# Expert weights into the keys' and values' memory: a fused attention and mixture-of-experts kernel

## Chip, cores and metric

One core of one Trainium2 chip runs the kernel. The metric is device time in microseconds (us), the median of several executions. A profiled execution has its own time, and the trace belongs to that one execution.

## What is computed

Inputs: q, k, v of 4 batches, 8 heads, 768 positions, 64 columns, float32; gate weights 512 x 8; expert weights w1 (8 x 512 x 1024) and w2 (8 x 1024 x 512); capacity 80. Attention with 4 sink positions and a window of 128 comes first, and its rows go through a router that gives each row to one expert:

```python
keep = is_sink | in_window
scores = np.where(keep, scores, -1000000000.0)
a = np.exp(scores - np.max(scores, axis=-1, keepdims=True))
a = a / (np.sum(a, axis=-1, keepdims=True) + 1e-09)
x = ...                       # rows: 3072 x 512, 8 heads side by side
expert_idx = np.argmax(x @ w_gate, axis=1)
for e in range(E):            # at most 80 rows of an expert, those of largest gate weight
    h = np.maximum(x[tok_idx] @ w1[e], 0.0)
    out[tok_idx] = gate_w[tok_idx, None] * (h @ w2[e])
```

All rows that no expert keeps are zero.

## The kernel before, in words

`attention_moe` does the work in one straight program (`any_window` is a general version behind a branch that these inputs don't take).

**Attention loop.** 48 ticks, 12 per batch. A tick takes two blocks of 128 queries by a pair of heads. Tick n computes scores on TensorE (`scores`, L504) into one PSUM bank a block; VectorE masks and takes the negated row maximum (`softmax`, L521 to L531); ScalarE takes exponentials with the row sum (`exps`, L541). One tick later the probabilities are transposed (`transposes`, L557) and copied by ScalarE (`keep_probs`, L569), GpSimd cuts them into two triangles (L577, L584), and two ticks later TensorE multiplies by the values (`weighted`, L592, L598). The sinks' values are kept in float32r with a remainder: `round_v` (L382) rounds them on ScalarE, `split_v` (L387) subtracts on GpSimd, 4 pieces a batch, in batch 0 within tick 1. The only table load of ScalarE stands ahead of its first exponential (L541).

Finished rows are turned back (L631), copied by ScalarE into one of two `xr` buffers (L636), scaled by GpSimd (L641) and stored to `x_rows` in DRAM (L645). Gate logits and keys follow, and VectorE compares each key with all earlier ones in pieces of 768 (`rank_compare`, L746, L749); this work goes on after the last tick.

**Order.** All of it is written by hand: `at(n, f)` puts a step at tick n and the loop issues the engines' instructions tick by tick. Loads and stores of the loop stand in one queue, SyncE's, which issues in order and stops at a transfer whose wait isn't over. Each transfer also waits for the one eight places ahead of it.

**Keys and values.** A batch's keys (`k`) and values (`v`) come from two rotating buffers each, in pool `ld` on the right side of memory. It closes after the last tick (`lctx.close()`, L904).

**Weights.** The 16 matrices (1 MB a half, 32 halves) are wanted in the order w1 of 0, w1 of 1, w2 of 0, w1 of 2, w2 of 1 and so on. They go to 17 places: `NA` = 6 in a pool that is there from the start, loaded from tick `W0` = 26 every `WD` = 3 ticks; `NB` = 7 in `ld`'s memory, issued together after the last tick (L905 to L908); `NC` = 4 in memory of the loop's other pools (L964 to L967). The last 15 halves replace used ones (`in_home`, L289 to L291).

**After the loop.** Ranks become row numbers (L978 to L996), GpSimd gathers each expert's 80 rows from `x_rows` (L1007), with 14 matmuls meanwhile that keep TensorE busy (L1005). Then, for expert e: `tokens` transposes its rows (L1037, copy L1039), `ffn1` multiplies by w1 (L1051, 128 matmuls: for each of 8 column groups all 4 row groups of w1), `ffn2` by w2 (L1066, 128 matmuls: for each of 4 column groups all 8 row groups), `rows` transposes back, scales and scatters to `out` (L1082 to L1094). TensorE's order is ffn1(e), tokens(e+1), rows(e-2), ffn2(e-1). A half of a weight matrix is half of its rows, so every column group reads both halves.

Of the kernel before, what the change touches and what calls it, by code (L numbers as in the profile page):

```python
# [8 lines left out]
F32 = mybir.dt.float32  # L9
F32R = mybir.dt.float32r  # L10
# [3 lines left out]
AF = mybir.ActivationFunctionType  # L14
# [5 lines left out]
B, H, S, D = 4, 8, 768, 64  # L20
# [215 lines left out]
Z0, ZD, W0, WD = 4, 1, 26, 3  # L236
# [7 lines left out]
def attention_moe(ctx: ExitStack, tc, q, k, v, n_sink, window, w_gate, w1, w2, capacity, q_t, k_t, v_t, vs_t, wg_t, out):  # L244
# [7 lines left out]
    NA, NB, NC = 6, 7, 4  # L252
# [31 lines left out]
    def load_weight():  # L284
        n = len(wtiles)
        which, e, half = wsrc[n]
        src = (w1, w2)[which][e].rearrange("(g c p) f -> g p c f", g=2, p=P)[half]

        k = n - NA - NB - NC  # L289
        in_home.append(n if k < 0 else in_home[1 + 7 * k // 4])  # L290
        pool, m = homes[in_home[n]]  # L291
        t = pool.tile([P, 2 * F], F32, tag=f"w{m}", name=f"w_{which}_{e}_{half}", bufs=1)
        nc.sync.dma_start(t.rearrange("p (c f) -> p c f", c=src.shape[1]), src)
        wtiles[(which, e, half)] = t

    zeros = const.tile([P, DM], F32, name="zeros")
    ve.memset(zeros, 0.0)

    with ExitStack() as actx:
# [60 lines left out]

        def load_k(b, pieces=1):
            ks[b] = ld.tile([P, NPAIR, NBLK * BLKW], F32, tag="k", name=f"k_{b}")
            n = NPAIR // pieces
            for i in range(pieces):
                nc.sync.dma_start(ks[b][:, i * n:(i + 1) * n], k_t[b][:, i * n:(i + 1) * n])

        def load_v(b, upto=NPB):

            if b not in vv:
                vst[b] = vst_rows[b % 2]  # L370
                vv[b] = ld.tile([P, NBLK, DM], F32, tag="v", name=f"v_{b}")
            for i in range(v_done.get(b, 0), upto):
                nc.sync.dma_start(vv[b][:, 2 * i:2 * i + 2], v_t[b][:, 2 * i:2 * i + 2])
                if i == 0:
                    nc.sync.dma_start(vst_raw, vs_t[b])
            v_done[b] = upto
# [3 lines left out]
        def round_v(b, m):  # L380
            a, hp = m // 2, slice(m % 2 * 2, m % 2 * 2 + 2)
            ac.copy(vst[b][0:SROWS, a, hp].bitcast(F32R), vst_raw[0:SROWS, a, hp])  # L382

        def split_v(b, m):

            a, hp = m // 2, slice(m % 2 * 2, m % 2 * 2 + 2)
            po.tensor_tensor(vst[b][32:SROWS, a, hp].bitcast(F32R), vst_raw[32:SROWS, a, hp], vst[b][32:SROWS, a, hp],  # L387
                             ALU.subtract)
# [9 lines left out]
        first_k = ks[0] = ld.tile([P, NPAIR, NBLK * BLKW], F32, tag="k", name="k_0")  # L398
# [380 lines left out]
        def at(n, f, *args):  # L779
            cal.setdefault(n, []).append((f, args))  # L780
# [7 lines left out]
        for n in range(NA):  # L788
            at(W0 + WD * n, load_weight)
        at((2, "pool"), make_experts)  # L790
# [13 lines left out]
        for m in range(4):  # L804
            at((1, "act mid"), round_v, 0, m)
            at((1, "pool"), split_v, 0, m)
# [50 lines left out]
        with tc.manual_schedule():  # L857
            n = 0
            while n <= END:
# [34 lines left out]
                run(n, "pe end")  # L894
                run(n, "act end")
# [6 lines left out]
                if n == END:  # L902

                    lctx.close()  # L904
                    wpool2 = fast.enter_context(tc.tile_pool(name="wpool2", bufs=1, side="right", reuse_waits="tile"))  # L905
                    homes += [(wpool2, m) for m in range(NB)]
                    for _ in range(NB):
                        load_weight()  # L908
# [54 lines left out]
    with ExitStack() as fctx:  # L963
# [7 lines left out]
        for e in range(E):  # L971
            xg[e] = sm.tile([CAP, DM], F32, name=f"xg_{e}")
# [68 lines left out]
        def ffn1(e):  # L1041
            need(0, e)
            x = xts.pop(e)
            h = wk.tile([P, HC, CAP], F32, tag="h", name=f"h_{e}")
            for half in range(2):
                ph = ps_h.tile([P, HC // 2, CAP], F32, tag="ph", name=f"ph_{e}_{half}")
                for f in range(HC // 2):
                    fc = half * (HC // 2) + f
                    for c in range(DC):
                        for m in range(2):  # L1050
                            pe.matmul(ph[m * D:(m + 1) * D, f], columns(0, e, c, fc * P + m * D),  # L1051
                                      x[:, c], start=(c == 0), stop=(c == DC - 1), skip_group_check=True)
                ac.activation(h[:, half * (HC // 2):(half + 1) * (HC // 2)], ph, AF.Relu)  # L1053
            hs[e] = h

        def ffn2(e, between=None):
# [5 lines left out]
            for dc in range(DC):  # L1062
                to = py if dc < DC // 2 else last
                for k in range(HC):
                    for m in range(2):
                        pe.matmul(to[m * D:(m + 1) * D, dc], columns(1, e, k, dc * P + m * D), h[:, k],  # L1066
                                  start=(k == 0), stop=(k == HC - 1), skip_group_check=True)
# [106 lines left out]
```

## Time and profile before

| | us |
|---|---|
| three timed executions | 322.2, 322.96, 324.96 (median 322.96) |
| the profiled execution | 321.46 |
| its span, first to last instruction | 319.7 |
| attention loop, first exponential to last tick's | 9.4 to 187 |
| ranks and row numbers | to 216.5 |
| gather, experts, last scatter | 216.5 to 319.7 |

A row of the profile names line, engine, operation, output and inputs. "issue" after an arrow is a wait for nothing that the profile shows. SPq is SyncE's queue. The granted TensorE clock stands as a share of 2.4 GHz.

### The profile page before, as it was taken

To read this page: it belongs to the slowest core of one execution; us is meant where nothing else is said; L and a number is where in the kernel's file an instruction comes from. 1 tells how busy PE (TensorE), PEld (TensorE's weight loads), DVE (VectorE), ACT (ScalarE), POOL (GpSimd) and SP (SyncE) were. 2 spreads that over 40 slices of the span, in tenths; PEclk is the share of its full clock that TensorE was granted. 3 is DMA by queue.
4 is the path that set the end of the run, shared out by engine and by line. 5 is a ranking of instruction groups with operands and counts; after the bars stand their busy time and mean duration, and the time that the engine had idled before them with its cause. 6 is when DMAs were issued, how large, how long until landed. Compare 5 with 4: busy or idle time off the path is not lost. (4 is left out here: it accounts for less than half of the span.)

```text
span 319.7 us, 11526 instructions
## 1 busy us (share of the span) xinstructions
PE 276.4 (86%) x4616; PEld 218.6 (68%) x4616; DVE 180.5 (56%) x576; ACT 159.1 (50%) x631; POOL 164.8 (52%) x365
## 2 busy tenths in 40 slices
PE   7498999999979999999999895745888989999792
PEld 2265776867767777777676673332788989998681
DVE  5345988777888989799989999970000000000001
ACT  0766897788968788777776661100111212111110
POOL 4396797769897588967667765507300111011001
PEclk9679999999999999999999999558999999999998
DMA  6999143699553899345260002999996696677501
GB/s 180 326 310 413 73 133 134 223 285 324 201 202 113 279 380 408 133 148 156 111 200 35 35 3 73 355 408 368 321 380 238 220 351 211 214 253 267 186 23 49
DMA packets 27115, 69.72 MB, mean 218 GB/s; under 512 B 2736, under 2 KB 3760, under 8 KB 26672
## 3 DMA queue, kind: packets, MB, share of 16 engines
q1 hardware_dynamic: 25744, 65.78, 59.5%
q0 software_dynamic: 1024, 2.62, 2.5%
q8 instruction: 38, 0.62, 0.8%
q10 hardware_dynamic: 288, 0.52, 0.4%
q14 instruction: 21, 0.17, 0.2%
HBM read 55.02 MB, written 13.89 MB: 216 GB/s over the span
## 5 line engine op out<-in xcount | busy, mean ns | idle before, releaser
L541 ACT ACTIVATE prob<-sc,nm 128x132 f32<-128x132 f32 (+1 forms) x192 | 69.0, 376 | 6.6 <-DVE nm L531 6.4
L504 PE MATMUL sc<-k,q 64*64 64x196 f32 (+2 forms) x768 | 48.4, 341 | 11.4 <-ACT prob L541 10.0
L1094 POOL DMA_INDIRECT out_dram<-y,idx x8 | 7.4, 921 | 81.8 <-ACT y L1083 71.6
L569 ACT COPY pt<-pp 128x512 f32<-128x512 f32 x48 | 28.1, 586 | 32.7 <-PE pp L557 24.1
L1039 DVE COPY xs<-px 128x320 f32<-128x320 f32 x8 | 3.9, 492 | 70.4 <-PE px L1037 70.4
L531 DVE TENSOR_REDUCE nm<-sc 128x2 f32<-128x264 f32 (+1 forms) x96 | 41.4, 431 | 3.3
L1051 PE MATMUL ph<-xs,w 128*64 128x80 f32 x1024 | 38.6, 233 | 5.2 <-issue 4.0
L524 DVE COPY_PREDICATED sc<-upper,sc 128x256 f32<-128x256 int8 x80 | 33.7, 421 | 14.0 <-PE sc L504 7.2
L504 PEld LDWEIGHTS sc<-k,q 64*64 64x64 f32 x768 | 21.6, 135 | 29.1 <-ACT prob L541 20.9
L1051 PEld LDWEIGHTS ph<-xs,w 128*64 128x64 f32 x1024 | 36.8, 137 | 6.4 <-issue 5.5
L1066 PE MATMUL py<-h,w 128*64 128x80 f32 x1024 | 38.4, 234 | 2.7 <-issue 2.0
L541 ACT ACTIVATION_READ_ACCUMULATOR prob<-sc,nm 128x1 f32 x192 | 40.3, 210 | 0.0
L1066 PEld LDWEIGHTS py<-h,w 128*64 128x64 f32 x1024 | 36.3, 137 | 4.9 <-issue 4.0
L598 PE MATMUL xp<-pt,v 128*64 128x128 f32 x384 | 37.5, 288 | 0.0
L577 POOL TENSOR_SCALAR_AFFINE_SELECT own<-pt 128x512 f32<-128x512 f32 (+1 forms) x48 | 28.7, 598 | 16.1 <-ACT pt L569 15.5
L749 DVE TENSOR_SCALAR_CACHE_REDUCE gt<-krow,keys 128x768 bf16<-128x768 f32 x36 | 35.5, 1004 | 0.0
L557 PE MATMUL pp<-ident,prob 128*128 128x128 f32 x192 | 32.3, 292 | 0.0
L598 PE MATMUL xp<-own,v 128*64 128x128 f32 x320 | 31.3, 274 | 0.0
L557 PEld LDWEIGHTS pp<-ident,prob 128*128 128x128 f32 x192 | 20.8, 144 | 13.9 <-issue 9.9
L1053 ACT ACTIVATE h<-ph 128x320 f32<-128x320 f32 x16 | 7.0, 438 | 44.1 <-PE ph L1051 44.1
L584 POOL TENSOR_SCALAR_AFFINE_SELECT pt<-pt 128x512 f32<-128x512 f32 (+1 forms) x48 | 27.2, 567 | 3.3
L641 POOL TENSOR_TENSOR xr<-xr,rs 128x512 f32<-128x512 f32 x24 | 25.6, 1069 | 6.0 <-ACT xr L636 5.7
(145 smaller groups left out, 461.6 us busy)
## 6 DMA issues: line engine op xcount, KB each, us to landing
w<-in_moe_w_dram SPq DMA_DIRECT2D x32, 1024.0 KB, 6.7
v<-in_v_t_dram SPq DMA_DIRECT2D x12, 512.0 KB, 7.5
out_dram<-zeros SPq DMA_DIRECT2D x24, 256.0 KB, 3.3
q<-in_q_t_dram SPq DMA_DIRECT2D x11, 512.0 KB, 7.2
x_rows<-xr SPq DMA_DIRECT2D x22, 256.0 KB, 2.2
k<-in_k_t_dram SPq DMA_DIRECT2D x3, 1584.0 KB, 9.0
k<-in_k_t_dram SPq DMA_DIRECT2D x1, 1056.0 KB, 9.7
vst_raw<-in_vs_t_dram SPq DMA_DIRECT2D x4, 256.0 KB, 6.2
```

What stands on the lines that cost most here:

```text
L504: pe.matmul(sc[u * D:(u + 1) * D, h, c0 + lo:c0 + hi], qs[g][r, hp, q0:q0 + D], ks[b][r, hp, k0 + lo:k0 + hi], start=True, stop=True, skip ...
L524: ve.copy_predicated(own, upper, sc[:, :, 0:P])
L531: ve.tensor_reduce(out=nm, in_=sc[:, :, lo_c:hi_c], axis=AX.X, op=ALU.max, negate=True)
L541: ac.activation(prob[:, a, h, p0:], sc[:, h, lo_c:hi_c], AF.Exp, bias=nm[:, h:h + 1], scale=1.0, accum_out=ssum[:, n, 2 * hp + h:2 * hp + ...
L557: pe.transpose(pp[:, a, h], prob[:, a, h, SINK:], ident)
L569: ac.copy(pt, st.pop((t, "pp")))
L577: po.affine_select(out=own[:, a0:], in_=pt[:, a0:], pattern=[[0, 2 - a0], [0, 2], [1, P]], compare_op=ALU.is_ge, fill=0.0, base=0, channel ...
L584: po.affine_select(out=pt[:, a0:], in_=pt[:, a0:], pattern=[[0, 2 - a0], [0, 2], [-1, P]], compare_op=ALU.is_gt, fill=0.0, base=0, channel ...
L598: pe.matmul(xp[h * D:(h + 1) * D, a * P:(a + 1) * P], val[:, (2 * hp + h) * D:(2 * hp + h + 1) * D], pr[:, a, h], start=False, stop=(a == ...
L749: ve.tensor_scalar(gt[:, 0:w], krow[:, c0:c0 + w], keys[:, i:i + 1], None, ALU.is_ge, ALU.add, accum_out=ra)
L1051: pe.matmul(ph[m * D:(m + 1) * D, f], columns(0, e, c, fc * P + m * D), x[:, c], start=(c == 0), stop=(c == DC - 1), skip_group_check=True)
L1066: pe.matmul(to[m * D:(m + 1) * D, dc], columns(1, e, k, dc * P + m * D), h[:, k], start=(k == 0), stop=(k == HC - 1), skip_group_check=True)
```

## The change

1. ScalarE's first instruction becomes an exponential of a zero (`first_exp`), and the table load stands ahead of that.
2. Batch 0's sink values are rounded and split on VectorE, at the end of tick 1, instead of on ScalarE and GpSimd.
3. Keys and values of a batch share one tile of a pool `kv` (two buffers). `NA` is 7 and `NB` 6: the pool from the start holds 7 halves, every 2 ticks from tick 26. Three halves go over batch 2's keys and values (tile `wkv`) at ticks 40, 42 and 44, two over batch 3's within tick 47, behind its last scores, and one after the last `weighted`. The last four (`NC`) stay where they were. To make room, the last expert's gathered rows use the tile `zeros`.
4. `ffn1` goes through all column groups with the first half of w1's rows, then with the second; `ffn2` likewise (not for the last expert). A used half is so released in the middle of a multiplication, the other at its end.

```diff
-Z0, ZD, W0, WD = 4, 1, 26, 3
+Z0, ZD, W0, WD = 4, 1, 26, 2
-    NA, NB, NC = 6, 7, 4
+    NA, NB, NC = 7, 6, 4
...
+    def kv_homes(n):
+        t = kv_tiles[B - 1] if n else kv.tile([P, NPAIR * NBLK * BLKW + NBLK * DM], F32, tag="kv", name="wkv")
+        homes.extend((None, t[:, m * 2 * F:(m + 1) * 2 * F]) for m in range(NB // 2))
...
+    first_exp = const.tile([P, 1], F32, name="first_exp")
+    ac.activation(first_exp, zeros[:, 0:1], AF.Exp)
...
+        at((NTK - 1, "act early"), kv_homes, 1)
+        for _ in range(NB // 2 - 1):
+            at((NTK - 1, "act early"), load_weight)
+
+        W1 = (B - 1) * NPB * NPAIR + 4
+        at(W1, kv_homes, 0)
+        for n in range(NB // 2):
+            at(W1 + WD * n, load_weight)
...
-        for m in range(4):
-            at((1, "act mid"), round_v, 0, m)
-            at((1, "pool"), split_v, 0, m)
+        for m in (0, 2, 1, 3):
+            at((1, "dve end"), round_v, 0, m, ve.tensor_copy)
+            at((1, "dve end"), split_v, 0, m, ve)
...
                 run(n, "pe end")
+                if n == END:
+                    load_weight()
...
-            xg[e] = sm.tile([CAP, DM], F32, name=f"xg_{e}")
+            xg[e] = sm.tile([CAP, DM], F32, name=f"xg_{e}") if e < E - 1 else zeros[0:CAP]
...
+            for c0 in range(0, DC, DC // 2):
+                for fc in range(HC):
+                    for c in range(c0, c0 + DC // 2):
+                        for m in range(2):
+                            pe.matmul(ph[fc // (HC // 2)][m * D:(m + 1) * D, fc % (HC // 2)],
+                                      columns(0, e, c, fc * P + m * D), x[:, c],
+                                      start=(c == 0 and fc % (HC // 2) == 0), stop=(c == DC - 1), skip_group_check=True)
...
+            steps = [(dc, range(k0, k0 + HC // 2)) for k0 in (0, HC // 2) for dc in range(DC)]
+            if between is not None:
+                steps = [(dc, range(HC)) for dc in range(DC)]
```

SyncE's queue from tick 42 to behind the last tick, before (`w` is a half of a weight matrix, `x_rows` a row store):

```order
L645 DMA x_rows<-xr_1_2826 128x512
L645 DMA x_rows<-xr_0_2968 128x512
L645 DMA x_rows<-xr_1_3120 128x512
L645 DMA x_rows<-xr_0_3263 128x512
L645 DMA x_rows<-xr_1_3393 128x512
L293 DMA w_2_0_3421<-in_moe_w_dram 128x2x1024
L293 DMA w_2_1_3423<-in_moe_w_dram 128x2x1024
L293 DMA w_1_0_3425<-in_moe_w_dram 128x4x512
L293 DMA w_1_1_3427<-in_moe_w_dram 128x4x512
```

The same stretch of the queue now, where `wkv` and `kv` are halves in the place of batch 2's and batch 3's keys and values:

```order
L296 DMA w_2_0_2645<-in_moe_w_dram 128x2x1024
L296 DMA wkv<-in_moe_w_dram 128x2x1024
L667 DMA x_rows<-xr_0_2772 128x512
L667 DMA x_rows<-xr_1_2833 128x512
L296 DMA wkv<-in_moe_w_dram 128x4x512
L667 DMA x_rows<-xr_0_2974 128x512
L296 DMA wkv<-in_moe_w_dram 128x4x512
L667 DMA x_rows<-xr_1_3127 128x512
L296 DMA kv_1960<-in_moe_w_dram 128x2x1024 x2
L667 DMA x_rows<-xr_0_3272 128x512
L296 DMA kv_1960<-in_moe_w_dram 128x4x512
L667 DMA x_rows<-xr_1_3403 128x512
```

Seven halves that stood behind the last row store stand ahead of it.

ScalarE's first instructions before:

```order
L541 ACT_TABLE_LOAD
L541 ACTIVATE prob_199,sum_201<-sc_108,nm_0_202 128x128 x2
L541 ACTIVATE prob_199,sum_201<-sc_109,nm_1_207 128x132 x2
L569 COPY pt_229<-pp_223 128x512
L382 CAST vst_110<-vst_raw 64x256 x4
L541 ACTIVATE prob_235,sum_201<-sc_108,nm_0_237 128x128 x2
```

And now:

```order
L311 ACT_TABLE_LOAD
L311 ACTIVATE first_exp<-zeros 128x1
L563 ACTIVATE prob_203,sum_205<-sc_113,nm_0_206 128x128 x2
L563 ACTIVATE prob_203,sum_205<-sc_114,nm_1_211 128x132 x2
L591 COPY pt_233<-pp_227 128x512
L563 ACTIVATE prob_235,sum_205<-sc_113,nm_0_237 128x128 x2
```

The four casts have gone from between the copy and tick 1's exponentials; VectorE has them, each with its subtraction, behind tick 1's maxima.

## Rows read from the trace of the kernel before

**Rows 1.** Page, part 2: the span in 40 slices, clock and DMA share
```profile
PEclk9679999999999999999999999558999999999998
DMA  6999143699553899345260002999996696677501
```

**Rows 2.** Windows: span; busy us of PE, PEld, DVE, ACT, POOL; clock, DMA, GB/s
```profile
112.00:128.00 16.00, 15.61 (x221) 11.54 (x214) 13.76 (x48) 13.58 (x56) 13.40 (x23) 1.00 1.01 393
...
180.00:198.00 18.00, 16.26 (x212) 12.71 (x204) 16.94 (x65) 9.42 (x36) 10.55 (x26) 1.00 0.09 31
```

**Rows 3.** Timeline of ScalarE, 8 to 17 us: start, duration, what, [idle before]
```profile
8.10 1.28 ACT L541 ACT_TABLE_LOAD   x1 [8.10 <-DVE nm L531]
9.40 0.37 ACT L541 ACTIVATE prob<-sc,nm 128x128 f32<-128x128 f32 x1
...
13.46 1.32 ACT L382 CAST vst<-vst_raw 64x256 fp32r<-64x256 f32 x4
14.68 0.36 ACT L541 ACTIVATE prob<-sc,nm 128x128 f32<-128x128 f32 x1
```

**Rows 4.** Timeline of VectorE, 6.5 to 17 us
```profile
8.66 0.43 DVE L531 TENSOR_REDUCE nm<-sc 128x2 f32<-128x264 f32 x1
...
16.36 0.49 DVE L521 COPY_PREDICATED_SCALAR sc<-upper,negc 128x256 f32 x1 [3.17 <-ACT stt L565]
```

**Rows 5.** Groups by form on VectorE: busy us, mean ns of one, idle before
```profile
L666 DVE TENSOR_TENSOR t<-pl,rs 128x128 f32<-128x128 f32 x11 | 3.1, 281 | 0.0
...
L983 DVE TENSOR_TENSOR hot<-slot_row,rank 128x640 bf16<-128x640 f32 x3 | 2.3, 821 | 0.0
...
L347 DVE CAST vst<-zeros 64x512 fp32r<-64x512 f32 x4 | 1.6, 472 | 0.0
```

**Rows 6.** Timeline of SyncE's queue, 196 to 210 us, weight tiles
```profile
198.22 11.50 SPq L293 DMA_DIRECT2D w<-in_moe_w_dram  x8
```

**Rows 7.** The same, 210 to 232 us
```profile
210.58 19.81 SPq L293 DMA_DIRECT2D w<-in_moe_w_dram  x4
```

**Rows 8.** Chain that ended last, from the gather on: start us, us, what
```profile
216.49 6.25 DMA xg<-x_rows,idx_in
...
233.85 0.88 issue
234.74 2.02 PE ph L1051 x52
...
237.19 2.63 PE py L1066 x71
239.82 1.21 issue
...
295.47 2.42 issue
```

**Rows 9.** DMA issues by line: the scatters of result rows; count, us to landing
```profile
out_dram<-y,idx POOLq DMA_INDIRECT x8, 3.6
```

**Rows 10.** Page, parts 1 and 3: instructions by engine; the instruction queue
```profile
PE 276.4 (86%) x4616; PEld 218.6 (68%) x4616; DVE 180.5 (56%) x576; ACT 159.1 (50%) x631; POOL 164.8 (52%) x365
...
q8 instruction: 38, 0.62, 0.8%
```

**Rows 11.** Waits of TensorE's weight loads, 223.5 to 243 us: total, times, longest
```profile
PEld ph L1051 <- issue: 3.0, 5, 1.0
PEld py L1066 <- issue: 1.4, 1, 1.4
```

**Rows 12.** The same, 243 to 302 us
```profile
PEld ph L1051 <- issue: 2.6, 1, 2.6
PEld py L1066 <- issue: 2.2, 7, 1.0
```

**Rows 13.** The same, 112 to 128 us
```profile
PEld sc L504 <- issue: 0.3, 2, 0.2
```

**Rows 14.** Timeline of SyncE's queue, 288 to 296 us
```profile
288.73 6.31 SPq L293 DMA_DIRECT2D w<-in_moe_w_dram  x3
```

More of the change, by code (lines that the diff above doesn't have):

```diff
@@ L291, in load_weight @@
         pool, m = homes[in_home[n]]
-        t = pool.tile([P, 2 * F], F32, tag=f"w{m}", name=f"w_{which}_{e}_{half}", bufs=1)
+        if pool is None:
+            t = m
+        else:
+            t = pool.tile([P, 2 * F], F32, tag=f"w{m}", name=f"w_{which}_{e}_{half}", bufs=1)
         nc.sync.dma_start(t.rearrange("p (c f) -> p c f", c=src.shape[1]), src)
         wtiles[(which, e, half)] = t
+    kv = fast.enter_context(tc.tile_pool(name="kv", bufs=2, side="right"))
+    kv_tiles = {}
+    def kv_homes(n):
+        t = kv_tiles[B - 1] if n else kv.tile([P, NPAIR * NBLK * BLKW + NBLK * DM], F32, tag="kv", name="wkv")
+        homes.extend((None, t[:, m * 2 * F:(m + 1) * 2 * F]) for m in range(NB // 2))
     zeros = const.tile([P, DM], F32, name="zeros")
     ve.memset(zeros, 0.0)
+    first_exp = const.tile([P, 1], F32, name="first_exp")
+    ac.activation(first_exp, zeros[:, 0:1], AF.Exp)
     with ExitStack() as actx:
@@ L359, in load_q, with alloc_kv @@
                 nc.sync.dma_start(qs[g][:, i * n:(i + 1) * n], q_t[g // NPB, g % NPB][:, i * n:(i + 1) * n])
+        def alloc_kv(b):
+            if b not in ks:
+                t = kv.tile([P, NPAIR * NBLK * BLKW + NBLK * DM], F32, tag="kv", name=f"kv_{b}")
+                kv_tiles[b] = t
+                ks[b] = t[:, 0:NPAIR * NBLK * BLKW].rearrange("p (h c) -> p h c", h=NPAIR)
+                vv[b] = t[:, NPAIR * NBLK * BLKW:].rearrange("p (c f) -> p c f", c=NBLK)
         def load_k(b, pieces=1):
-            ks[b] = ld.tile([P, NPAIR, NBLK * BLKW], F32, tag="k", name=f"k_{b}")
+            alloc_kv(b)
             n = NPAIR // pieces
@@ L367, in load_v @@
         def load_v(b, upto=NPB):
-            if b not in vv:
+            if b not in vst:
                 vst[b] = vst_rows[b % 2]
-                vv[b] = ld.tile([P, NBLK, DM], F32, tag="v", name=f"v_{b}")
+                alloc_kv(b)
             for i in range(v_done.get(b, 0), upto):
@@ L378, in attention_moe, with round_v, split_v @@
         v_done = {}
-        def round_v(b, m):
+        def round_v(b, m, copy=ac.copy):
             a, hp = m // 2, slice(m % 2 * 2, m % 2 * 2 + 2)
-            ac.copy(vst[b][0:SROWS, a, hp].bitcast(F32R), vst_raw[0:SROWS, a, hp])
-        def split_v(b, m):
+            copy(vst[b][0:SROWS, a, hp].bitcast(F32R), vst_raw[0:SROWS, a, hp])
+        def split_v(b, m, eng=po):
             a, hp = m // 2, slice(m % 2 * 2, m % 2 * 2 + 2)
-            po.tensor_tensor(vst[b][32:SROWS, a, hp].bitcast(F32R), vst_raw[32:SROWS, a, hp], vst[b][32:SROWS, a, hp],
+            eng.tensor_tensor(vst[b][32:SROWS, a, hp].bitcast(F32R), vst_raw[32:SROWS, a, hp], vst[b][32:SROWS, a, hp],
                              ALU.subtract)
@@ L397, in attention_moe @@
         first_q = qs[0] = ld.tile([P, NPAIR, 2 * P], F32, tag="q", name="q_0", bufs=3)
-        first_k = ks[0] = ld.tile([P, NPAIR, NBLK * BLKW], F32, tag="k", name="k_0")
+        alloc_kv(0)
+        first_k = ks[0]
         for i in range(NPAIR):
@@ L904, in attention_moe @@
                     lctx.close()
[L905 to L908, printed above, removed]
                 n += 1
@@ L1044, in ffn1 @@
             h = wk.tile([P, HC, CAP], F32, tag="h", name=f"h_{e}")
-            for half in range(2):
[L1046 to L1053, printed above, removed]
+            ph = [ps_h.tile([P, HC // 2, CAP], F32, tag="ph", name=f"ph_{e}_{half}") for half in range(2)]
+            for c0 in range(0, DC, DC // 2):
[5 more added lines that the diff above has]
+                                      start=(c == 0 and fc % (HC // 2) == 0), stop=(c == DC - 1), skip_group_check=True)
+            for half in range(2):
+                ac.activation(h[:, half * (HC // 2):(half + 1) * (HC // 2)], ph[half], AF.Relu)
             hs[e] = h
@@ L1061, in ffn2 @@
             last = ps_h.tile([P, HC // 2, CAP], F32, tag="ph", name=f"py2_{e}") if e == E - 1 else py
-            for dc in range(DC):
+            steps = [(dc, range(k0, k0 + HC // 2)) for k0 in (0, HC // 2) for dc in range(DC)]
+            if between is not None:
+                steps = [(dc, range(HC)) for dc in range(DC)]
+            for dc, some in steps:
                 to = py if dc < DC // 2 else last
-                for k in range(HC):
+                for k in some:
                     for m in range(2):
                         pe.matmul(to[m * D:(m + 1) * D, dc], columns(1, e, k, dc * P + m * D), h[:, k],
-                                  start=(k == 0), stop=(k == HC - 1), skip_group_check=True)
+                                  start=(k == 0 and (between is not None or dc == 0)), stop=(k == HC - 1),
+                                  skip_group_check=True)
                 if dc == DC // 2 - 1 and between is not None:
```

## The prediction

> **What bounds the kernel now.** I read the slices first, because the change moves transfers [rows 1]. A slice is 8 us. The DMA digits are 0 in slices 22 to 24, 168 to 192 us, and 9 in slices 26 to 30, 200 to 240 us. A window gives the empty stretch in GB/s: 31 from 180 to 198 us [rows 2]. So the loop's end leaves the memory path empty, and what follows it overfills it. The reason stands in SyncE's queue: eight weight tiles are issued from 198.22 us on, which takes 11.50 us where one issue alone takes under half a microsecond, and four more from 210.58 us [rows 6, 7].
>
> The second view is the chain of waits. From 216.49 us it is the gather of the first expert's rows, 6.25 us, and behind it TensorE alone, with pieces called "issue" between its matmuls: 0.88, 1.21 and 2.42 us are three of them [rows 8]. The weights of experts 0 and 1 have long been in memory then (loaded within the loop), so the first two are no waits for weights. Their distance says what they are. Between the ends of the 0.88 and the start of the 1.21 stand 52 + 71 matmuls and four transposes, 127 in all [rows 8]. A matmul is two instructions (a weight load and itself), which makes some 254. One DMA queue of kind "instruction" brought 38 packets, 0.62 MB, so 16 KB each [rows 10]; TensorE has 4616 matmuls and as many weight loads, 243 instructions for each packet. I read the pieces as instruction packets that come late behind weight tiles. The 2.42 us one fits: three halves were issued from 288.73 us on, within 6.31 us [rows 14].
>
> In the loop before that TensorE, VectorE and ScalarE are all nearly full (15.61, 13.76 and 13.58 of 16 us, [rows 2]), each tick waiting for the one before it. A shift of its first ticks goes through to its end; I see no transfer that holds it at a fixed time.
>
> **1. Table load and sink values.** Before, ScalarE stands until the first maximum at 8.10 us, then loads the table for 1.28 us, and the first exponential begins at 9.40 [rows 3]. With the load under the initial idle time the first begins at 8.10; but tick 0's second unit has its maximum only at 8.66 + 0.43 = 9.09 us [rows 4], against the 10.10 at which its exponential began, so what passes on is 10.10 - 9.14 = 0.96 us. The Trainium skill (ScalarE: Activation LUTs, What ACT_TABLE_LOAD costs) counts a drain of about 1.38 us on top of the load, 2.66 us in all. The rows show no such drain: 9.40 follows 8.10 + 1.28. By the page the first unit alone would gain 1.4 us more, and the second, held by its maximum, nothing.
>
> The four casts (13.46 to 14.78) stand between the probabilities' copy and tick 1's exponentials at 14.68 [rows 3]; that copy ends with the first cast's start or just behind, so some 1.1 to 1.2 us more, together 2.1. VectorE pays instead. A cast of 64x512 takes 472 ns, so 64x256 some 0.3 us; a subtraction lies between the products of 128 and of 640 columns, 281 and 821 ns, so about 0.4 [rows 5]. Four pairs are 2.8 us; the ends are 4 x (0.24 + 0.28) = 2.1, with half the cast and the smaller product, and 4 x (0.47 + 0.82) = 5.2. VectorE stood idle for 3.17 us to 16.36 [rows 4]. Shifted by 2.1 us, its next work comes at 14.3, and the pairs run from about 12 to 14.8: 0.5 us late at that point, but the next exponential waits for a copy behind TensorE's transposes, which is later still. GpSimd loses its four splits, which stood ahead of its triangles.
>
> What can eat part of it is the clock. PEclk is 6 and 7 in the second and third slice [rows 1]: TensorE runs at 1.2 GHz, half, until about 20 us, and if it rises no sooner, work pulled ahead of that point runs at half speed. About 2 us of it would cost up to 1.3. Bounds 0.7 (or minus 1, if VectorE's 5.2 decides) and 2.5; I take **1.6 us**.
>
> **2. Weights ahead.** Seven halves go from behind the last row store to ticks 38 to 49. They fall in the stretch of 31 GB/s. Seven are 7.3 MB, 19 us at the 393 GB/s of a full stretch (112 to 128 us, [rows 2]), and nothing waits for them there. Left between loop and gather are four, whose memory comes free no sooner than now: one at the end of the 11.50 us of [rows 6], three at 210.58 [rows 7], less the shift of 1.6. Three take 8 us, so they end near 217, and the gather begins at 216.49 - 1.6 = 214.9: it still meets 2 us of them, not 20.
>
> *Gather.* 6.25 us now. The scatters of equal rows, on an emptier path, land after 3.6 us [rows 9]. All of that difference would be 2.65, none of it 0. With 2 us shared, I take **1.8 us**.
>
> *Late packets, first stretch.* From 223.5 to 243 us the weight loads of TensorE wait 3.0 + 1.4 = 4.4 us for "issue" [rows 11]. About 0.8 belongs to the start (the copy of the rows). Of the 3.6 left, with a replacement tile now and then in place of twelve tiles in a row, I take 3.0.
>
> *Row halves, second stretch.* From 243 to 302 us they wait 2.6 + 2.2 = 4.8 [rows 12], of which some 0.8 are ends of a stage. The long ones follow pairs of halves released together, as at 288.73 [rows 14]. With halves released by turns, 2.3 us apart, each 1 MB has its 2.7 us nearly to itself. Not all pairs part (the last three halves still come within 8 us), so of 4.0 I take 2.6. Together **5.6 us**; the ends are 0 (packets as late as now) and 7.6. Number and kind of the matmuls stay, and the first Relu's wait moves from half to three quarters of `ffn1`, ahead of nothing that it delays.
>
> *What it could cost.* Row stores stand behind weights in the one queue. The tightest is that of tile 21, behind one half: up to 2.7 us later, and the copy of tile 23 waits for its buffer. That copy is wanted only for tile 23's own store, while VectorE still has comparisons to do, so nothing. Tick 40's tile waits for batch 2's last `weighted`, at tick 37; tick 47's two wait for scores of the same tick, and behind them stands only a row store two ticks from its use. Keys and values of batch 3 have one half more ahead of them, 2.7 us, and are used 8 ticks later.
>
> **Sum.** 1.6 + 1.8 + 5.6 = 9.0 us. The profiled execution took 321.46 (span 319.7 and 1.76 around it), which becomes 312.5. It lies 1.5 below the median of the timed ones, so I forecast 322.96 - 9.0 = 314.0 us. Its own range is 309 to 317.
>
> **Rivals.**
>
> *A. Only part of the packets are helped.* 15 of 32 halves are still loaded beside the experts, with the same bytes a microsecond from 243 on. If the second stretch keeps its 4.0 and the gather gains 0.8, what is left is 1.6 + 0.8 + 3.0 = 5.4: 317.6 us. For it: one packet meets one tile just as it meets two, by chance of phase. Against: in 243 to 302 most boundaries passed without a wait, since 14 halves left a longest wait of 2.6 and one of 1.0.
>
> *B. The "issue" pieces are something else.* The order of TensorE's own work, say, and they stay. Then start and gather remain, 3.4 us: 319.6 us. For it speaks the Trainium skill (Runtime: NRT & Kernel Launch, Instruction fetch mechanics), by which blocks of 16 KB are fetched while the one before is executed, and the fetch is mostly hidden. The block size agrees with the row of 16 KB a packet; that it is hidden doesn't agree with pieces that recur 127 matmuls apart.
>
> *C. The late packets move into the loop.* Ticks 26 to 49 take seven more halves, and TensorE gets about nine packets there. If each came 1.2 us late (between the 0.88 and the 2.42 of [rows 8]), the loop would lose 10.8 us. It decides once a packet is late by more than the reserve of the loop: there some 2500 matmuls run in 200 us, so a packet lasts about 10 us, against 2.02 + 2.63 and the transposes, 5 us, beside the experts [rows 8, 10]. With the gains of 9.0 the time would be 324.8 us, slower. Against it: from 112 to 128 us the path is full at 393 GB/s [rows 2], and the score matmuls' weight loads wait 0.3 us in all for "issue" [rows 13].
>
> *D. More than forecast.* The clock rises sooner, the gather lands like a scatter and hardly a packet is late: 2.5 + 2.6 + 7.0 = 12.1, so 310.9 us.
>
> **Chances.** The forecast 0.50, A 0.22, D 0.12, B 0.11, C 0.05. Range 308.5 to 319.5: it holds the forecast, A, D, and the near edge of B. A measurement of this kernel can tell about 1%, 3.2 us. The forecast, A and D are faster by over that; B, 3.4 us, is at the border, so I give half of it to no change, with some of A's lower end: faster 0.86, same 0.10, slower 0.04.
>
> **What would show it.** In the profile after: the first exponential at about 8.1 us and tick 1's at 12.6; DMA digits well over 0 in slices 22 to 25 and lower ones in slices 26 and 27; the gather's piece of the chain at 4 to 5 us; no "issue" piece over 0.5 us in the first two experts, and at most one over 1 us later. The step on the packets is wrong if those pieces stay as long with an emptier path; the step on the start, if the first tick at full clock isn't 1 us earlier; the whole, if the last tick's exponentials come later than 185 us.

## The result, and the profile after

Thirteen executions of each kernel: 318.88 us (317.45 to 320.19) now, 321.89 (319.01 to 324.96) before; the ratio is 0.9914, 95% interval 0.9887 to 0.9941. The change gains 0.9%, some 2.8 us, where 9.0 were forecast. The time lies within the range of 308.5 to 319.5, at its slow end.

Where the gain came and went, by the two profiled executions (span 319.7 before, 317.8 now; times in us from the span's start):

| | before | after | ahead of before |
|---|---|---|---|
| last tick's first exponential | 185.44 | 185.89 | -0.45 |
| first gather starts | 216.49 | 216.07 | 0.42 |
| first `px` matmul | 222.78 | 220.49 | 2.29 |
| `px` of expert 2 | 236.69 | 238.47 | -1.78 |
| `px` of expert 7 | 288.91 | 287.94 | 0.97 |
| last scatter starts | 315.37 | 312.99 | 2.38 |
| end of the span | 319.7 | 317.8 | 1.9 |

So the gather came out at the size forecast, the start gained nothing, and between the first two `px` rows 4.07 us were lost where part of the 3.0 was to be won. The slices (as [rows 1]):

```profile
PEclk9759999999999999999999999756789999999998
DMA  7999234599562799884725283983257795878501
```

The empty slices 22 to 24 are in use and the overfull ones have gone. But PEclk is 5 in the third slice (7 before), and 7, 5, 6, 7, 8 in slices 26 to 30, where it was 5, 5, 8 and then full. Windows of after (as [rows 2]):

```profile
20.00:22.00 2.00, 2.00 (x15) 1.41 (x15) 1.53 (x5) 0.27 (x2) 1.84 (x5) 0.50 1.00 310
22.00:24.00 2.00, 2.00 (x19) 1.55 (x22) 0.13 (x1) 2.00 (x10) 1.39 (x3) 0.50 0.94 234
...
180.00:198.00 18.00, 16.08 (x210) 12.76 (x211) 17.00 (x65) 9.80 (x38) 10.28 (x25) 1.00 0.46 161
...
221.00:226.00 5.00, 2.58 (x52) 2.18 (x52) 0.46 (x1) 0.00 (x0) 3.78 (x5) 1.00 0.45 128
226.00:233.00 7.00, 5.89 (x80) 5.72 (x80) 0.00 (x0) 0.82 (x2) 0.57 (x3) 0.53 0.13 38
```

From 180 to 198 us the path now carries 161 GB/s instead of 31, and the loop pays nothing for it: from tick 5 on each tick takes what it took before, to 0.02 us. From 221 to 226 us, though, TensorE is busy for half of the time, and from 226 to 233 it runs at 1.2 GHz. That stretch in the chain of waits (as [rows 8]):

```profile
215.83 4.83 PE warm L1033 x14
220.66 0.28 PE px L1065 x4
220.94 0.63 issue
221.56 1.99 PE ph L1079 x47
223.55 1.05 issue
224.60 0.36 PE ph L1079 x4
224.96 0.39 issue
225.34 0.23 PE ph L1079
225.57 0.49 issue
226.06 0.37 PE ph L1079 x4
226.43 1.05 issue
227.47 5.10 PE ph L1079 x71
232.58 0.74 PE px L1065 x4
```

The gather is no longer what TensorE waits for: `px` follows the warm matmuls. The late packets of before (0.88 and 1.21 us) have gone. In their place the first `ffn1` stops four times, 2.98 us in all, and its last 71 matmuls take 5.10 us at half clock, where 69 took 2.66. That is the whole loss of 4.1 us: the stops cost 2.98 where this stretch had 1.61 before (0.39, 0.34 and 0.88), the half clock costs 2.4 in the 71 matmuls and 0.3 in `px`. These stops are not late packets: the trace has no landing on the instruction queue between 216.17 and 229.56 us, whereas the pieces of 0.88, 1.21 and 2.42 us of before each ended 1.3 to 1.4 us behind one. Behind it TensorE's weight loads wait less (243 to 299 us, as [rows 12]): 1.6 us for "issue", against 4.8.

```profile
PEld py L1100 <- issue: 0.9, 5, 0.2
PEld ph L1079 <- issue: 0.7, 1, 0.7
```

The start, VectorE from 10 to 18 us (as [rows 4]):

```profile
10.47 0.43 DVE L553 TENSOR_REDUCE nm<-sc 128x2 f32<-128x264 f32 x1
12.79 0.28 DVE L403 CAST vst<-vst_raw 64x256 fp32r<-64x256 f32 x1 [1.89 <-DMA vst_raw<-in_vs_t_dram]
13.11 0.41 DVE L408 TENSOR_TENSOR vst<-vst_raw,vst 32x256 fp32r<-32x256 f32 x1
...
13.88 1.30 DVE L408 TENSOR_TENSOR vst<-vst_raw,vst 32x256 fp32r<-32x256 f32 x1
...
16.98 0.49 DVE L543 COPY_PREDICATED_SCALAR sc<-upper,negc 128x256 f32 x1
```

The first exponential begins at 7.12 us, 2.3 sooner, and tick 1's at 10.72, 4.0 sooner. Then VectorE stands 1.89 us for the transfer of `vst_raw` (issued at 5.04, landed at 12.77), works on the pairs until 16.95, and tick 2's mask, whose scores were done at 13.2, comes at 16.98. Tick 2's first exponential begins at 17.97, 0.8 us sooner than before (18.73): 3.2 of the 4.0 us have gone. The clock stays at half until 25.0 us (20.3 before), and from there to the first exponential of tick 4 8.5 us pass instead of 7.0: the rest goes too.

### The profile page after: what moved, and what is told of

Its sections match the earlier page's. It is cut to its first block, busy times and chain, and to the rows that moved or that the text cites. A ratio compares the mean times of both kernels' runs of the same rounds, so it can differ in the third digit from the quotient of the medians.

```text
span 317.8 us, 11525 instructions
## 1 busy us (share of the span) xinstructions
PE 279.2 (88%) x4616; PEld 222.6 (70%) x4616; DVE 184.2 (58%) x584; ACT 158.2 (50%) x628; POOL 162.7 (51%) x361
## 5 line engine op out<-in xcount | busy, mean ns | idle before, releaser
L563 ACT ACTIVATE prob<-sc,nm 128x132 f32<-128x132 f32 (+1 forms) x192 | 69.1, 376 | 15.0 <-DVE nm L553 14.8
L526 PE MATMUL sc<-kv,q 64*64 64x196 f32 (+2 forms) x768 | 48.8, 344 | 10.7 <-ACT prob L563 9.5
L526 PEld LDWEIGHTS sc<-kv,q 64*64 64x64 f32 x768 | 21.9, 136 | 28.1 <-ACT prob L563 21.4
L620 PE MATMUL xp<-pt,kv 128*64 128x128 f32 x384 | 37.9, 291 | 0.0
L1079 PE MATMUL ph<-xs,w 128*64 128x80 f32 x704 | 29.5, 244 | 4.8 <-issue 4.2
L1079 PEld LDWEIGHTS ph<-xs,w 128*64 128x64 f32 x704 | 28.0, 146 | 5.8 <-issue 4.8
L620 PE MATMUL xp<-own,kv 128*64 128x128 f32 x320 | 31.6, 276 | 0.0
L785 PE MATMUL bank_t<-gt,pick_row 128*128 128x384 bf16 (+2 forms) x92 | 22.1, 328 | 3.9 <-DVE gt L771 3.4
L1100 PE MATMUL py<-h,w 128*64 128x80 f32 x640 | 24.4, 234 | 0.5 <-issue 0.5
## 6 DMA issues: line engine op xcount, KB each, us to landing
kv<-in_k_t_dram SPq DMA_DIRECT2D x3, 1584.0 KB, 11.3
```

The lines of the kernel that those rows point to most:

```text
L526: pe.matmul(sc[u * D:(u + 1) * D, h, c0 + lo:c0 + hi], qs[g][r, hp, q0:q0 + D], ks[b][r, hp, k0 + lo:k0 + hi], start=True, stop=True, skip ...
L563: ac.activation(prob[:, a, h, p0:], sc[:, h, lo_c:hi_c], AF.Exp, bias=nm[:, h:h + 1], scale=1.0, accum_out=ssum[:, n, 2 * hp + h:2 * hp + ...
L620: pe.matmul(xp[h * D:(h + 1) * D, a * P:(a + 1) * P], val[:, (2 * hp + h) * D:(2 * hp + h + 1) * D], pr[:, a, h], start=False, stop=(a == ...
L1079: pe.matmul(ph[fc // (HC // 2)][m * D:(m + 1) * D, fc % (HC // 2)], columns(0, e, c, fc * P + m * D), x[:, c], start=(c == 0 and fc % (HC ...
```

## Experiments

All times are medians; a ratio is to the kernel before, in executions on the same chip. Differences between two changed kernels are differences of medians; for raw_first and spaced_gathers against the changed kernel the ratios give the same to 0.2 us.

### The start

**act_split**: part 2 undone.

```diff
-            at((1, "dve end"), round_v, 0, m, ve.tensor_copy)
-            at((1, "dve end"), split_v, 0, m, ve)
+            at((1, "act mid"), round_v, 0, m)
+            at((1, "pool"), split_v, 0, m)
```

> The changed kernel with part 2 undone: batch 0's sink values are rounded on ScalarE and split on GpSimd again; the early table load, the weights ahead and the row halves stay. Theory 1 (VectorE stands at its first sink cast until the transfer of `vst_raw` lands, 12.79 us in the changed kernel, and tick 2's mask, whose scores end at 13.2 us, starts behind the four pairs at 16.98): tick 2's exponentials begin at 15.5 to 16.5 us instead of 17.97, the last tick's 1.5 to 2.5 us sooner than the changed kernel's 185.9, and the time is 316.5 to 317.5 us. Rival (the clock sets it: TensorE at half clock from 11.4 to 25.0 us takes any gain back): tick 2 is sooner, but from tick 5 on the ticks stand within 0.5 us of the changed kernel's, and the time is 318 to 320 us.

318.32 us, ratio 0.9887 (0.9799 to 0.9975). Tick 2 begins at 17.5, not at 15.5 to 16.5: now ScalarE stands for the same transfer, and tick 1 behind it:

```profile
10.23 0.59 ACT L591 COPY pt<-pp 128x512 f32<-128x512 f32 x1 [1.24 <-PE pp L579]
12.19 1.32 ACT L403 CAST vst<-vst_raw 64x256 fp32r<-64x256 f32 x4 [1.37 <-DMA vst_raw<-in_vs_t_dram]
13.41 0.36 ACT L563 ACTIVATE prob<-sc,nm 128x128 f32<-128x128 f32 x1
```

The last tick came at 186.05, but this execution also ran at half clock from 93.3 to 96.7 us, where tick 23 took 6.36 us instead of 4.8; up to tick 23 it was 1.0 us ahead of the changed kernel and 0.5 ahead of the one before. Neither difference is clear of the spread: seven executions that start as the changed kernel does (it, no_halves, late_gathers, spaced_gathers, many_small, warm_11 and warm_20) begin tick 23 at 89.95 to 92.37 us and the last tick at 183.37 to 185.89, median 185.27. What both theories had overlooked is that ScalarE would wait for the same transfer.

**raw_first**: the changed kernel, batch 0's `vst_raw` issued ahead of its first `v`.

```diff
             for i in range(v_done.get(b, 0), upto):
+                if i == 0 and b == 0:
+                    nc.sync.dma_start(vst_raw, vs_t[b])
                 nc.sync.dma_start(vv[b][:, 2 * i:2 * i + 2], v_t[b][:, 2 * i:2 * i + 2])
-                if i == 0:
+                if i == 0 and b > 0:
```

> The changed kernel with one transfer moved: `vst_raw` of batch 0 is issued ahead of the first piece of `v` instead of behind it. Theory 1 (VectorE waits for `vst_raw`): its wait of 1.89 us ahead of the first sink cast shrinks by 1 us or more, the four pairs end 1 us or more sooner than 16.95, tick 2's mask with them, and the loop ends about 1 us sooner; 317.5 to 318.5 us. If the wait for `vst_raw` is not what holds tick 2, tick 2's first exponential stays at 18.0 us.

315.87 us, ratio 0.9816 (0.9752 to 0.988), 3.0 us below the changed kernel, three times what was expected. The wait has gone (VectorE from 10 to 15 us):

```profile
10.11 0.43 DVE L555 TENSOR_REDUCE nm<-sc 128x2 f32<-128x264 f32 x1
10.46 0.28 DVE L405 CAST vst<-vst_raw 64x256 fp32r<-64x256 f32 x1
...
14.42 0.49 DVE L545 COPY_PREDICATED_SCALAR sc<-upper,negc 128x256 f32 x1
```

Tick 2 begins at 15.4, the clock is full from 20.9 us on, and the last tick begins at 182.56, 3.3 us sooner: more than the wait, since the clock's rise came along. raw_spaced, with the same start, begins it at 183.00; both are sooner than any of the seven named above. The first expert still loses what it lost.

**raw_act**: both edits, `vst_raw` first and part 2 undone.

> raw_first with part 2 undone: `vst_raw` of batch 0 is loaded ahead of the first values, and the sink values are rounded on ScalarE and split on GpSimd as before the change. It tells what part 2 itself is worth once nobody waits for that transfer. Theory 1 (the transfer was the wait; the pairs' 3.9 us on VectorE remain between tick 1's maxima and tick 2's mask): ScalarE's casts start right behind its copy, tick 2's first exponential begins at 14.0 to 15.0 us instead of raw_first's 15.4, and the time is within 1 us of raw_first's 315.9, on either side. If moving the pairs to VectorE is worth the 1.1 us that it was forecast to be, this one is 317 us.

311.10 us, ratio 0.9656 (0.9629 to 0.9683). Tick 2 begins at 17.7 and the last tick at 184.22, 1.7 us behind raw_first (1.3 in the pair raw_spaced and raw_act_spaced, below): with the data there, VectorE is the better place for the pairs in both pairs of traces, though the differences are smaller than the spread of 2.5 us among the seven. The time is lower all the same, since this kernel's first expert has no stops (below): from the first `px` to that of expert 2 pass 11.31 us, against 18.07 in raw_first.

**table_only**: the kernel before with part 1 alone.

> The kernel before with part 1 alone, the early table load. As forecast (0.96 us passes on, from the second unit's maximum): the last tick's exponentials begin at 184.4 to 184.6 instead of 185.44, and ScalarE's casts still stand between the copy and tick 1's exponentials. If ScalarE now waits at the casts for `vst_raw`, whose transfer lands at 12.7 us, tick 1 begins at 13.4 to 13.8 us, and no more than that 0.9 to 1.3 us is to be had from any earlier start.

321.48 us, ratio 1.0007 (0.9963 to 1.0052): nothing. Yet the loop gained: tick 1 begins at 13.23, the last tick at 183.73, 1.7 us sooner than in the profile of before (1.3 sooner in table_warm, below, which has the same start). Where TensorE stands for the gather the clock falls, and the first `ffn1` takes 7.06 us; but that is made up, since the late packet of 0.88 us doesn't come, and `px` of expert 7 is still 1.9 us ahead (286.97 against 288.91). The gain goes behind that, where a late packet is followed by half clock from 295.6 to 299.0 us and the last 104 matmuls of an `ffn1` take 5.30 us instead of 3.82:

```profile
217.00:221.00 4.00, 1.55 (x8) 0.76 (x7) 0.00 (x0) 0.00 (x0) 3.07 (x4) 0.93 1.06 383
221.00:229.00 8.00, 7.37 (x128) 7.16 (x130) 0.49 (x1) 0.44 (x1) 3.29 (x5) 0.60 1.04 331
```

```profile
293.31 2.59 issue
295.90 5.30 PE ph L1053 x104
```

### The first expert

**late_gathers**: the changed kernel, six of eight gathers later.

```diff
-        for e in range(E):
+        for e in range(2):
+            gather(e)
...
             ffn1(e)
+            if e + 2 < E:
+                po.tensor_copy(probe, hs[e][:, HC - 1, 0:1])
+                gather(e + 2)
```

> The changed kernel, but only experts 0 and 1 are gathered at once; each later gather waits on GpSimd for the hidden layer of the expert two before it. It tells what stops TensorE within the first `ffn1` (1.05, 0.39, 0.49 and 1.05 us of 'issue' from 223.55 to 227.47 us, with the clock at half from 226.4 to 233.2 us behind it). Theory G (the row gathers under way do it): the pieces go, the clock stays full, expert 0's first multiplication takes 4.5 us as later ones do, and the time falls by 4 to 5 us, to 314 to 315 us. Theory P (it is a place in TensorE's instructions): the pieces stay at the same matmuls, 47 to 57 of 128, and the time stays within 1 us of the changed kernel's 318.9.

316.84 us, ratio 0.9828 (0.9753 to 0.9902). The first `ffn1` has no stop, the clock is full from 219.5 us on, and `px` of expert 2 comes at 231.97, 6.5 us sooner than in the changed kernel. But stops came up elsewhere, two at each of the four places where now a gather and a scatter follow one another on GpSimd (0.30 us apart):

```profile
255.24 0.94 POOL L1133 DMA_INDIRECT out_dram<-y,idx  x1 [0.30 <-issue]
256.02 0.37 PE L1104 MATMUL py<-h,kv 128*64 128x80 f32 x4 [0.29 <-issue]
...
256.77 1.41 PE L1104 MATMUL py<-h,w 128*64 128x80 f32 x35 [0.32 <-issue]
```

**spaced_gathers**: no indirect transfer near another, once the first three are out.

```diff
-        for e in range(E):
+        for e in range(3):
+            gather(e)
...
             ffn1(e)
+            if e < 2:
+                po.tensor_copy(probe, hs[e][:, HC - 1, 0:1])
+                gather(e + 3)
...
                 ffn2(e - 1)
+            if 1 < e < E - 3:
+                po.tensor_copy(probe, yts[e - 1][:, DC - 1, 0:1])
+                gather(e + 3)
```

> The changed kernel with row gathers spread out: three at once, the next two behind the hidden layers of experts 0 and 1, the last three behind the outputs of experts 1 to 3, some 4 us away from every scatter. In late_gathers TensorE stopped twice for 0.5 us each time a gather and a scatter followed one another on GpSimd within 0.3 us (244.93 and 245.68 us among them), and not at the gathers that stood alone at 227.13 and 232.88. Theory G1 (it takes indirect transfers issued one right behind another): no such piece is left anywhere, the clock stays full from the warm matmuls on, and the time is 312.5 to 314 us. Rival G2 (every gather beside running matmuls costs TensorE about 1.1 us): five such pieces stay and the time is 316.5 to 318 us, as late_gathers' 316.8.

312.12 us, ratio 0.9699 (0.9659 to 0.9739): 6.8 us below the changed kernel, a little more than expected. The weight loads of the first two experts wait for "issue" once, 0.8 us at the copy of the first rows, and the clock is full:

```profile
219.00:226.00 7.00, 6.37 (x141) 5.63 (x139) 0.49 (x1) 0.79 (x2) 0.54 (x3) 1.00 0.13 39
226.00:232.00 6.00, 5.42 (x143) 5.21 (x144) 0.76 (x2) 0.96 (x3) 1.30 (x3) 1.00 0.83 279
```

From the first `px` to that of expert 2 pass 11.31 us, against 17.97 in the changed kernel. So the stops, and the half clock behind them, were the price of gathers beside the first expert; five gathers alone cost nothing (G2 falls).

**raw_spaced**: spaced_gathers with raw_first's order.

> spaced_gathers with raw_first's order of the first loads. If the two losses are separate, one at the start and one in the first expert, their gains add: raw_first stood 3.0 us below the changed kernel, so this stands 3.0 us below spaced_gathers, 309.5 to 311 us under theory G1. If the clock or the loop's end swallows one of them, it is no more than 1 us below the better of the two.

310.82 us, ratio 0.9636 (0.9586 to 0.9686), only 1.3 below spaced_gathers, where 3.0 were expected; with four executions each (308.86 to 312.07 and 311.29 to 313.67) even the 1.3 is not clear of the noise. The last tick begins 2.2 us sooner and `px` of expert 2 comes 2.5 sooner, but two packets are late that weren't (1.05 us at 255.51 and 0.68 at 266.36 in its chain): a shift moves the packets against the weight tiles.

**raw_act_spaced**: raw_act with the spread gathers.

> raw_act with the spread gathers of spaced_gathers. raw_act's profile shows no 'issue' piece in the first expert although its eight gathers are issued at once. Theory G3 (back-to-back gathers stop TensorE in some programs and not in others, and raw_act escaped): there is nothing to gain, and the time is within 1 us of raw_act's 311.1. Theory G1 as it stood (they always do, and raw_act's profiled execution is the exception among its runs): 3 us or more below raw_act, 308 us or less.

310.99 us, ratio 0.9647 (0.9577 to 0.9717): the same as raw_act. So raw_act's executions do run without stops, although its eight gathers go out at once, at the same distances as in the changed kernel. Eight gathers beside TensorE are needed for the stops, but they are not enough.

**many_small, warm_11, warm_20**: the changed kernel with 11 warm matmuls and 48 tiny ones, with 11, and with 20.

> The changed kernel with 11 warm matmuls instead of 14 and 48 tiny ones (8 columns) behind them, so that TensorE has passed 90 more instructions when the first `ffn1` begins, at about the same time. In the four kernels whose first `ffn1` stops, it stops after 43 to 53 matmuls, and it goes on in steps of about 0.72 us until 11.4 us behind the first gather's start. Theory S (while the gathers are issued TensorE gets its instructions at a slow rate, and it stops when it has used up some 100 that it had in store): it now stops sooner, within the first 15 matmuls of `ffn1`, and still until 11.4 us. Rival T (the time is what counts): it stops again from 7.1 us behind the first gather's start on, whatever instruction stands there.

> The changed kernel with 11 warm matmuls instead of 14: TensorE begins the first expert as soon as its rows have landed, if that is sooner than 4.4 us behind the first gather's start. Theory S (TensorE has some 100 instructions in store and gets more at a slow rate while the gathers are issued): the stops begin after 43 to 53 matmuls of the first ffn1 again, sooner in time by what the first px is sooner. Rival T (the time counts): from 7.1 us behind the first gather's start on, after more matmuls. If no stop is left, it is neither count nor time alone.

> The changed kernel with 20 warm matmuls: the first px begins 1.2 us later, 5.6 us behind the first gather's start. Theory S: the stops begin after 43 to 53 matmuls, 8.3 us behind the first gather's start, and end at 11.4 us: two or three are left, and the clock may stay full; 316 to 318 us. Rival T: from 7.1 us on, after some 10 matmuls, and as long as before; 319 to 320 us.

317.53, 317.73 and 315.48 us (two executions each). many_small has no stop in the first expert, against both theories; its clock was at half there, from 221.2 to 224.6 us. In the other two the weight loads of the first `ffn1` first stop after 45 and 42 matmuls (47 with 14 warm ones; 40 in table_warm with 28), and in time 6.7 and 8.7 us behind the first gather's start (7.3; 9.4): the count within `ffn1` moves little, the time moves with the start of `ffn1`, as theory S forecast. S itself isn't shown: by its store of instructions many_small had to stop sooner, and a place in TensorE's instructions that stops it only while gathers are issued would look the same. The last stop ends at 11.3 us in both (11.4 in the changed kernel). warm_20:

```profile
220.68 1.71 PE L1079 MATMUL ph<-xs,w 128*64 128x80 f32 x42 [0.63 <-issue]
223.40 0.38 PE L1079 MATMUL ph<-xs,w 128*64 128x80 f32 x4 [1.02 <-issue]
224.14 0.23 PE L1079 MATMUL ph<-xs,w 128*64 128x80 f32 x1 [0.36 <-issue]
224.85 4.62 PE L1079 MATMUL ph<-xs,w 128*64 128x80 f32 x81 [0.48 <-issue]
```

**table_warm**: table_only with 28 warm matmuls.

> table_only with 28 warm matmuls instead of 14. In table_only the loop ends 1.7 us sooner than in the kernel before (183.73 against 185.44), yet the time is the same: TensorE stands from 217.5 to 220.9 us for the gather, its clock is at half from 220.5 to 227.3 us, and the first ffn1 takes 7.06 us instead of 6.1. Theory K (the clock falls because TensorE stood in that wait): 14 more warm matmuls at 0.2 us fill the wait, the clock stays full, the first two experts come 2.5 to 3.5 us sooner than in table_only, and the time is 318 to 319.5 us. Rival (the clock falls for another reason, or the warm matmuls delay the first px): 321 to 322 us again.

324.16 us, ratio 1.0068 (1.0028 to 1.0108), slower than before. The clock did stay full from 218.0 us on, as theory K has it, but two stops came up in the first `ffn1` (0.64 and 1.06 us), `px` began 0.45 us later behind the first gather, and late packets took more (pieces of 1.54, 0.99 and 3.17 us in its chain). Filling the wait kept the clock there; the gain went all the same.

### The later experts

**no_halves**: the changed kernel with part 4 undone.

> The changed kernel with part 4 undone: both multiplications go through a column group's whole depth again, and both halves of a matrix come free together. Theory 1 (halves in pairs make instruction packets late): between 243 and 302 us TensorE's weight loads wait for 'issue' 3 us longer than in the changed kernel, pieces of over 0.5 us come back 1.3 us behind the end of a packet of the instruction queue, and the time is 321 to 322.5 us. Rival (the weights loaded ahead did it): the stretch stays as in the changed kernel, and the time is 318.5 to 319.5 us.

322.10 us, ratio 0.9978 (0.994 to 1.0017): without row halves the whole change is worth nothing. From 243 to 304 us its weight loads wait 5.7 us for "issue" (1.6 with them):

```profile
PEld ph L1079 <- issue: 4.2, 3, 2.7
PEld py L1094 <- issue: 1.5, 7, 0.3
```

The other traces bear it out, so it isn't the phase of one run: from `px` of expert 2 to the end of the span, ten kernels with row halves take 78.8 to 81.8 us (late_gathers, with its stops beside the scatters, 84.4), and the four that load all weights without them 83.1 to 88.1.

**no_late_loads**: the kernel before without its last 15 weight loads.

```diff
+        if k >= 0:
+            wtiles[(which, e, half)] = wtiles[wsrc[in_home[n]]]
+            return
         pool, m = homes[in_home[n]]
```

> The kernel before without its last 15 weight loads: a matrix that would replace a used one is not loaded, and its expert multiplies by what stands there. Left out: those 15 MB; TensorE's instructions stay. Theory 1 (TensorE's long 'issue' pieces are instruction packets that come late behind weight tiles): from 243 us on no piece of over 0.3 us is left but those at the ends of a stage, packets of the instruction queue land within 1 us of one another's spacing, and the stretch from the end of expert 0's second multiplication (243.2) to the start of the last one (302.3) falls from 59.1 to 55 us; about 318 us. Rival (the pieces belong to the order of TensorE's own work): they stay where they are, and the stretch stays at 59 us.

315.15 us, ratio 0.9783 (0.9746 to 0.9819). TensorE's chain from 241 us on runs without a gap, an expert in 9.87 us, where before took 10.3 on the mean:

```profile
241.05 4.43 PE ph L1054 x128
245.48 0.43 PE px L1040 x4
245.91 0.44 PE pry L1085 x4
246.35 4.58 PE py L1069 x128
250.93 4.43 PE ph L1054 x128
255.35 0.43 PE px L1040 x4
```

The stretch falls from 59.1 to 54.3 us (241.05 to 295.39). The order of TensorE's work is as before, so the long pieces behind 241 us belong to the weight transfers: rival B falls.

## Why the prediction was wrong, step by step

**Start, 1.6 us forecast, -0.45 in the profile.** The step that failed is "I see no transfer that holds it at a fixed time", and with it "the pairs run from about 12 to 14.8": `vst_raw` was issued at 5.04 us and landed at 12.77. Before, the casts stood later than that (13.46), so the transfer hid behind work that the change moved away. Part 1 did pass on something of the order forecast (0.96): table_only was 1.7 us and table_warm 1.3 ahead of before at the last tick, in one execution each. Part 2's term, 1.1 us, was nothing or a loss while the load stood where it was (tick 23 came 1.0 us later than in act_split, within the spread), and is a gain of 1.3 to 1.7 with the load moved (raw_first and raw_spaced against raw_act and raw_act_spaced). The -0.45 is one execution; by the median of the seven (185.27, against 185.44 before and 185.20 in no_late_loads, which starts as before) the start gained nothing. The pairs took 4.2 us instead of 2.8, within the bounds. That the clock might take up to 1.3 was in the text; it took 1.5, for full clock came later (25.0 us, 20.3 before) and not at the same time. warm_20 shows how little a sooner first tick was worth: its first exponential came 0.9 us later than in the changed kernel's trace (7.98 against 7.12), VectorE waited for no transfer, the clock was full from 20.0 us on, and its last tick began 2.5 us sooner (183.37).

**Gather, 1.8 forecast, 1.9 measured** (6.29 to 4.42 from its start to `px`). The number is right in part by luck. The forecast left the gather 2 us of weight tiles to share the path with and so a landing after some 4.45 us; the path beside it carried 59 GB/s instead of 373, and the first gather landed after 3.3 us. What then held `px` until 4.42 were the 14 warm matmuls, which the forecast didn't count; with 11 of them it began after 4.07 (warm_11).

**First stretch, +3.0 forecast, -2.6 measured** (from the first `px` to the end of expert 0's second multiplication, 243.19 before and 243.54 now; it is -4.1 up to `px` of expert 2, and the 1.21 us that no longer come lie behind that). The step that failed is that the stretch was summed from the waits seen before, with nothing new to come. The 0.88 and the 1.21 us did go. But an earlier first `ffn1` runs beside the last gathers instead of behind them, and TensorE stops there, and its clock falls; without the stops (spaced_gathers) the way from the first `px` to that of expert 2 takes 11.31 us instead of 17.97. Two small pieces of before, 0.39 and 0.34 us, which "about 0.8 belongs to the start" passed over, were by their place (they end 10.1 and 10.9 us behind the first gather's start, and no instruction packet landed between 217.52 and 233.33 us) the same stops, at their tail end. "What is late next" was asked of transfers, and not of GpSimd.

**Second stretch, 2.6 forecast, 3.2 measured** in the waits. Right, and by the mechanism named: packets come late behind weight tiles, and halves by turns help; no_halves gives it all back, no_late_loads takes all of it away. Rival A's argument, chance of phase, held too: in raw_spaced two late packets took back 1.7 of the 2.5 us that it was ahead. But that the measured time lies between A's 317.6 and B's 319.6 us speaks for neither: A kept the second stretch's waits and B all of the pieces, and neither had a loss in the first expert. That it lies within the range is luck.

**Costs.** Row stores, keys and the loop paid nothing; rival C falls. D fell with the start.

The sum: 1.6 became -0.45, 3.0 became -2.6; 1.8 came out at 1.9, and 2.6 at 3.2 in the waits, 3.4 by start and end times. No term had the 0.9 us won between the last tick and the first gather (30.1 to 30.2 us in every kernel with the change, 30.9 to 31.1 in those without; which part does it is not shown), nor the 1.1 lost behind the start of the last `ffn2`, where one more late packet stands (0.45 us). So -0.45 + 0.9 + 1.9 - 2.6 + 3.4 - 1.1 make some 2 us, the 1.9 of the span. With the raw values loaded first and the gathers spread it stands at 310.8 us (raw_spaced), 3.6% below the kernel before and, by the two ratios, 2.8% below the changed one.

What stays open is what else the stops take. It is no full memory path: in the 11.5 us behind the first gather's start it carried 112 GB/s in the changed kernel and 367 in table_warm, and both stopped. Of the kernels with all gathers at once, eight had them and four had none. Three of these four (many_small, table_only, no_late_loads) ran at half clock in part of that stretch, where TensorE takes its instructions more slowly (128 matmuls of the first `ffn1` in 5.9 to 7.1 us, against 4.65); raw_act ran at full clock, and nothing in its trace tells why it was spared.

## What to carry to other kernels

Work that is moved ahead meets the transfer that its old place hid: read the landing time of each input of a moved instruction, not only the engine's idle time. Where a wait ends sooner, look at what else runs in the stretch into which the next stage slides, off the bound engine too, since GpSimd's transfers and the clock can take the gain. And where packets and tiles meet by phase, a microsecond won ahead of them is not a microsecond at the end: take the wait's cause away (no burst of loads, no burst of gathers), rather than shift it.

## What was not expected of the hardware

- TensorE stops beside indirect transfers that GpSimd issues back to back (0.30 us apart): for 0.2 to 1.1 us each time, with 1 to 6 matmuls in between, on steps of about 0.72 us. It went on until 1.3 us behind the end of the last one's issue where there were eight, and 0.6 us where there were two (late_gathers). Beside those that stood alone (five in spaced_gathers) it didn't stop, and in four traces with all eight at once it didn't either.
- Where TensorE stood for an instruction packet, it went on 1.3 to 1.4 us behind the packet's landing: packets that landed at 233.3 and 239.7 us in the kernel before were followed by the next weight loads at 234.74 and 241.03. In 28 such waits of nine traces it was 1.2 to 1.5 us.
- VectorE's subtraction of 32x256 took 0.41 us, but 1.30 (in the changed kernel) and 1.14 (raw_first) where GpSimd scaled a block of 128x1024 at the same time.
